# Four small moves in a sparse-attention and MoE kernel: two key loads between two row moves, three attention products one group sooner

## The chip, the cores and the metric

The kernel runs on one core of one Trainium2 chip. The metric is the device time of one execution in microseconds (us). Inside the core, TensorE (PE in the profile) multiplies, VectorE (DVE), ScalarE (ACT) and GpSimd (POOL) work on tiles, and SyncE (SP) only issues transfers (DMAs). Each engine takes its instructions strictly in the order in which the program wrote them, and waits at an instruction until what it needs has arrived.

## What is computed

Sparse attention over 4 batches, 8 heads, 768 positions and 64 features per head, and then a two-layer expert on the result. Each query sees the keys less than 16 positions away, and one summary key and value for each block of 32 positions (the maximum of the keys, the mean of the values):

```python
k_sum = k.reshape(B, H, nb, block, D).max(axis=3)
v_sum = v.reshape(B, H, nb, block, D).mean(axis=3)
scores_l = where(abs(pos_q - pos_k) < 16, scale * q @ k.T, -1e9)
scores_s = scale * q @ k_sum.T + log(block)
a = softmax(concat([scores_l, scores_s]))
x = a @ concat([v, v_sum])               # then heads side by side: 3072 x 512
h = x @ w_in                             # 512 -> 2048
out = (h * sigmoid(beta * h)) @ w_out    # 2048 -> 512
```

## The kernel before

**Tiles.** The 8 heads are taken as 4 pairs. The 768 queries of a batch are 12 tiles of 64, in two halves u of 6. For one tile the scores stand with the keys on the partitions: rows 0 to 95 are the window of 96 keys, rows 96 to 119 the 24 summary keys. `scores` (L323) fills a half for both heads of a pair in one of the three double PSUM banks `big`, ACT takes the exponential of it into a tile `e` (`weigh`, L332), and DVE multiplies `e` by the band mask (`mask_e`, L337). `av_mm` (L406) then multiplies 24 small tiles of a half: the slice of `e` is the loaded weight, and the values with a column of ones stream through; in the text a pair's two halves are AV(pair, 0) and AV(pair, 1). `norm` (L432) on DVE divides by the sum (a reciprocal and a product) and writes `xn`, and `x_dma` (L465) is a transposing DMA on ACT's queue from `xn` into `xT`, where the expert's first product reads it.

**Values.** A window of an even query tile lies at other rows than that of an odd one, so the values exist twice: `ve` for even tiles, and `vo`, the same rows shifted by 64. For batches 1 to 3, `v_cast` (L343, POOL) casts a pair into `ve`, and `v_odd_dma` (L354), the "row moves" of the pair, are two DMAs on SP's queue: L355 copies rows 64 to 127 of `ve` to rows 0 to 63 of `vo`, L356 copies rows 0 to 31 to rows 64 to 95. The summary values come from TensorE (`vm_all`, L384), and `spread` (L394, DVE) copies them into rows 96 to 127 of `vo` and of `ve`, two pairs at a time: spread(0) for pairs 0 and 1, spread(1) for pairs 2 and 3, each as two copies into `vo` and then two into `ve`. Row move L355 of a pair reads rows of `ve` (64 to 127) that spread overwrites (96 to 127), so the copies of spread(1) into `ve` wait until the row moves L355 of pairs 2 and 3 have landed.

**Loads.** `key_load` (L94) brings one pair's keys of a later batch (384 KB) by SP's queue into a staging tile `kst`; POOL and DVE cast it during the next stage.

**Order.** Nothing is scheduled by a tool: `run` (L551) takes a list of main steps and a list of side steps with positions, and writes a side step with position x behind main step floor(x), in rising order of x. In the stage around the change the main steps are the 24 groups of the second expert product of batch 0 (`o_atom`, L534): 6 tiles of 128 tokens, 4 groups each, 4 products of 128x512 in a group. The side steps are all of batch 1's attention: casts and row moves of the values, the eight score halves, masks, spreads, the four AV blocks (`av_at`, L680, pair 0 at 12.12 in `big[0]`, pairs 1, 2, 3 at 16.1 to 16.3 in `big[1]`, `big[2]`, `big[0]`), their x transposes, and the key loads of batch 2. The first expert product of batch 1 (`h_tile`, L516) follows on TensorE.

Of the kernel before, what the change touches and what calls it, by code (L numbers as in the profile page):

```python
# [11 lines left out]
def kernel(  # L12
# [57 lines left out]
    def pair(a, b, g):  # L70
        return a[b, 2 * g:2 * g + 2]
# [22 lines left out]
    def key_load(b, g):  # L94
        f = stage.tile([RK, 2, CK * D], f32, name="kst", tag="kst")
        stg[("k", b, g)] = f
        nc.sync.dma_start(out=f[:], in_=pair(k, b, g).rearrange("h (p c) d -> p h (c d)", c=CK))
# [186 lines left out]
    def km_pe(g, ks):  # L284
        key_max_win(g)
        key_sums(ks, g)
# [50 lines left out]
    def mask_e(b, g, u):  # L337
        e = et[(b, g, u)]
        return nc.vector.tensor_mul(out=e.rearrange("p h (m q) -> p h m q", q=QT), in0=e.rearrange("p h (m q) -> p h m q", q=QT),  # L339
                             in1=mask[:, None, u * HT:(u + 1) * HT, :].to_broadcast([P, 2, HT, QT]))  # L340
# [53 lines left out]
    def spread(gg):  # L394
        r = slice(NK, P)
        s = slice(2 * gg, 2 * gg + 2)
        for tt in (vo, ve):
            for h in range(2):
                nc.vector.tensor_copy(out=tt[r, s, h * J6:(h + 1) * J6, 0:D],
                                      in_=vm_sb[r, h, s, None, :].to_broadcast([P - NK, 2, J6, D]))  # L400
# [5 lines left out]
    def av_mm(b, g, u, t):  # L406
        tv = t[:, 0:AVW].rearrange("p (j h e) -> p j h e", j=3, h=2)
        e = et[(b, g, u)]
        for j in range(3):
            J = 3 * u + j  # L410
            for h in range(2):
                for par in range(2):
                    lo = (2 * j + par) * QT
                    nc.tensor.matmul(tv[par * QT:(par + 1) * QT, j, h], e[:, h, lo:lo + QT],  # L414
                                     (vo if par else ve)[:, g, h * J6 + J, 0:D + 1], start=True, stop=True)
# [16 lines left out]
    def norm(b, g, t, us):  # L432
        t = t[:, 0:len(us)]
        n = len(us)
        if us[0] == 0:
            xn[(b, g)] = xp.tile([P, J6, 2, D], bf16, name="xn", tag="xn")
        x = xn[(b, g)]
        tv = t[:, :, 0:AVW].rearrange("p k (a e) -> p k a e", e=D + 1)
        r = xp.tile([P, n, 6], f32, name="r", tag="r")
        nc.vector.reciprocal(out=r[:], in_=tv[:, :, :, D])  # L440
        nc.vector.tensor_mul(out=x[:, 3 * us[0]:3 * us[0] + 3 * n].rearrange("p (k j) h d -> p k (j h) d", k=n),  # L441
                             in0=tv[:, :, :, 0:D], in1=r[:, :, :, None].to_broadcast([P, n, 6, D]))
# [22 lines left out]
    def x_dma(b, g):  # L465
        nc.scalar.dma_start_transpose(out=xT[:, g, :].rearrange("p (j t) -> p j t", j=J6),
                                    in_=xn[(b, g)].rearrange("p j h d -> p (j h d)"))
# [83 lines left out]
    def run(main, sides):  # L551
        sides = sorted(sides, key=lambda x: x[0])
        for i, f in enumerate(main):
            f()
            while sides and sides[0][0] < i + 1:
                sides.pop(0)[1]()
        for _, f in sides:
            f()
# [84 lines left out]
    s = []  # L643
    wo = []

    def scale4(p, eng=None):
        for n in range(4 * p, 4 * p + 4):
            scale_w_out(n, eng)
# [26 lines left out]
    s = [(6, lambda: scale4(1)), (12, lambda: scale4(2)), (.5, clear_kw), (14, lambda: km_pe(0, nc.gpsimd))]  # L675
# [4 lines left out]
    def av_at(b, s, pos, bufs):  # L680
        for g in range(G):
            def av(g=g):
                for u in range(2):
                    av_mm(b, g, u, big[bufs[g]][:, u])
                norm(b, g, big[bufs[g]], [0, 1])
                if g == 0 and b > 1:
                    for u in range(2):
                        last_mask[b] = mask_e(b, G - 1, u)
            s.append((pos[g], av))

    def x_pe2(b, g, t):
        t = t.bitcast(bf16)[:, 0, 0:S]
        x = xn[(b, g)]
        for j in range(J6):
# [3 lines left out]
    s = [(.05, exp_table), (.15, lambda: scale4(3)), (.2, lambda: km_pe(1, nc.gpsimd)),  # L698
         (.3, lambda: km_pe(2, nc.gpsimd)), (3.52, lambda: km_pe(3, nc.gpsimd))]
# [10 lines left out]
    s.append((9.06, lambda: vm_all(one[1], [dve_cp] * 4)))  # L710
    s.append((9.1, lambda: spread(0)))
    s.append((9.11, lambda: spread(1)))
    av_at(1, s, [12.12, 16.1, 16.2, 16.3], [0, 1, 2, 0])
    for g in range(G):
        s.append(((12.2, 16.35, 16.4, 16.5)[g], lambda g=g: x_dma(1, g)))
    for g in range(G):
        s.append(((3.56, 3.561, 3.562, 3.563)[g], lambda g=g: key_load(2, g)))
    run(main, s)


# [3 lines left out]
    for b in range(1, B):  # L724
        n = b + 1
        s = []
# [22 lines left out]
        s = [((x[0] - 16) * 1.2, x[1]) for x in late]  # L749
# [53 lines left out]
```

## Time and profile before

| | us |
|---|---|
| median of 3 runs | 214.59 |
| fastest and slowest of them | 213.94 and 214.81 |
| the profiled execution, its whole time | 214.21 |
| its span, first to last instruction | 212.5 |
| TensorE busy in the span | 205.4 |
| VectorE, ScalarE, GpSimd busy | 110.0, 106.8, 53.8 |

Positions in the trace are us from the start of the span. A row of the timeline gives start, length, engine, line and operation of neighbouring instructions taken together, and in brackets how long the engine was idle before them and what ended that. For a DMA the row's length is the time that the issuing engine spent on it; how long after the start of the issue the data had arrived is told apart from it, as "to landing".

### The profile page before, as it was taken

What the parts mean: (1) busy time and instruction counts of PE and PEld (TensorE: products, weight loads), DVE (VectorE), ACT (ScalarE), POOL (GpSimd) and SP (SyncE); (2) the same over time, 40 slices, a digit from 0 to 9 for tenths busy, and PEclk for the clock granted to TensorE, in tenths of its full rate; (3) what the DMA queues carried; (4) which work ended last, traced back from release to release, by engine and by line L of the source; (5) the groups of instructions that cost most, each with busy time, mean ns of one, the idle gap of its engine ahead of it and who ended that gap; (6) DMA issues with size and microseconds to landing.
All of it is one profiled execution on the core that took longest, in us unless ns stands there. A gap on an engine that the chain in (4) does not pass through costs nothing.

```text
span 212.5 us, 5283 instructions
## 1 busy us (share of the span) xinstructions
PE 205.4 (97%) x2231; PEld 120.6 (57%) x2231; DVE 110.0 (52%) x251; ACT 106.8 (50%) x142; POOL 53.8 (25%) x85
## 2 busy tenths in 40 slices
PE   7997999999999999999999999999999999999993
PEld 7776766665455455665555456654554556654452
DVE  5669675398758623942798217635887100002121
ACT  2478586686756027669541066676450076640000
POOL 7949970003411203543103013343000000000000
PEclk9999999999999999999999999999999999999999
DMA  6999999999969989999579999999445400001212
GB/s 125 188 220 176 173 201 206 207 207 170 204 195 238 258 204 220 207 208 161 134 215 258 224 206 233 158 219 179 137 123 121 142 0 0 0 3 49 99 52 96
DMA packets 74534, 34.08 MB, mean 160 GB/s; under 512 B 61440, under 2 KB 70032, under 8 KB 74512
## 3 DMA queue, kind: packets, MB, share of 16 engines
q1 hardware_dynamic: 57440, 24.05, 51.8%
q0 software_dynamic: 7440, 7.34, 21.6%
q10 hardware_dynamic: 9632, 2.37, 7.5%
q8 instruction: 17, 0.28, 0.6%
q14 instruction: 5, 0.04, 0.1%
HBM read 27.37 MB, written 6.29 MB: 158 GB/s over the span
## 4 chain that ended last, share of the span: by engine, by line
PE 89%; DVE 3%; DMA 3%; POOL 2%; issue 1%; POOLq 0%; DVEq 0%
PE one L526 39%; PE big L509 29%; PE big L495 5%; PE one L501 3%; DMA qrow<-in_q_dram 3%; PE big L414 2%; PE big L328 2%; PE big L501 2%; PE big L276 1%; DVE qn L247 1%; PE one L388 1%; POOL krow L87 1%; PE big L315 0%; PE big L260 0%; DVE ve L344 0%
## 5 line engine op out<-in xcount | busy, mean ns | idle before, releaser
L526 PE MATMUL one<-w_out_sb,h_sb 128*128 128x512 bf16 (+1 forms) x400 | 85.8, 371 | 0.0
L521 ACT ACTIVATE h_sb<-big,beta_sb 128x768 bf16<-128x768 f32 x48 | 42.6, 900 | 47.5 <-PE big L509 47.5
L509 PE MATMUL big<-xT,w_in_sb 128*128 128x384 bf16 x384 | 63.1, 326 | 0.0
L526 PEld LDWEIGHTS <-h_sb 128*128 128x128 bf16 x400 | 38.1, 98 | 41.3 <-issue 0.2
L509 PEld LDWEIGHTS <-w_in_sb 128*128 128x128 bf16 x384 | 37.6, 98 | 25.3 <-issue 0.2
L247 DVE COPY o_sb<-one 128x512 f32<-128x512 f32 x19 | 13.1, 690 | 45.2 <-PE one L526 45.0
L335 ACT ACTIVATE e<-big,bias 128x768 bf16<-128x768 f32 x32 | 26.5, 897 | 16.1 <-PE big L328 13.5
L339 DVE TENSOR_TENSOR e<-e,mask 128x768 bf16<-128x768 bf16 x27 | 15.4, 594 | 14.8 <-ACT e L335 14.6
L247 DVE COPY kw<-kT 128x960 bf16<-128x960 bf16 (+1 forms) x16 | 10.2, 683 | 14.2 <-DMA kT<-kn 14.2
L344 POOL CAST ve<-vst 128x832 bf16<-128x832 f32 x15 | 13.6, 905 | 13.7 <-DMA vst<-in_v_dram 10.4
L475 POOL CAST qn<-qst 128x768 bf16<-128x768 f32 x8 | 6.6, 826 | 29.4 <-DMA qst<-in_q_dram 27.7
L241 POOL COPY kw<-km 128x288 bf16<-128x288 bf16 x12 | 7.1, 603 | 26.9 <-DVE km L233 26.9
L441 DVE TENSOR_TENSOR xn<-big,r 128x768 bf16<-128x768 f32 (+1 forms) x13 | 12.0, 927 | 0.4
L495 PE MATMUL big<-xT,w_in_sb 128*128 128x384 bf16 x64 | 11.5, 326 | 0.0
L233 DVE TENSOR_REDUCE km<-kw 128x24 bf16<-128x768 bf16 x12 | 11.3, 947 | 0.3
L641 ACT ACTIVATE h_sb<-big,beta_sb 128x384 bf16<-128x384 f32 x16 | 8.1, 579 | 2.7 <-PE big L495 2.7
L483 POOL CAST kn<-kst 96x1024 bf16<-96x1024 f32 x4 | 4.1, 1037 | 21.1 <-DVE e L339 19.1
L501 PEld LDWEIGHTS <-w_in_sb 128*128 128x128 bf16 x64 | 6.2, 98 | 4.1
L543 PE MATMUL one<-blank 128*128 128x128 bf16 (+1 forms) x98 | 7.0, 235 | 1.3 <-DVE blank L125 1.3
L501 PE MATMUL one<-xT,w_in_sb 128*128 128x384 bf16 x44 | 8.1, 326 | 0.0
L495 PEld LDWEIGHTS <-w_in_sb 128*128 128x128 bf16 x64 | 5.9, 98 | 3.6
L247 DVE COPY kw<-big 128x960 bf16<-128x960 bf16 (+1 forms) x8 | 5.3, 733 | 4.7 <-PE big L276 4.7
(126 smaller groups left out, 186.9 us busy)
## 6 DMA issues: line engine op xcount, KB each, us to landing
out_dram<-o_sb SPq DMA_DIRECT2D x23, 256.0 KB, 2.5
vst<-in_v_dram SPq DMA_DIRECT2D x13, 336.0 KB, 4.6
kst<-in_k_dram SPq DMA_DIRECT2D x8, 384.0 KB, 5.7
qst<-in_q_dram SPq DMA_DIRECT2D x8, 384.0 KB, 4.1
w_in_sb<-in_moe_w_in_dram POOLq DMA_DIRECT2D x4, 512.0 KB, 7.2
w_out_sb<-in_moe_w_out_dram POOLq DMA_DIRECT2D x4, 512.0 KB, 14.3
vo<-ve SPq DMA_DIRECT2D x12, 107.2 KB, 2.4
vst<-in_v_dram SPq DMA_DIRECT2D x3, 416.0 KB, 6.9
```

What stands on the lines that cost most here:

```text
L233: nc.vector.tensor_reduce(out=km[g][:, NK:NK + nb].rearrange("p (m n) -> p m n", n=2), in_=kw[g][:, :, W:W + QT].rearrange("p m (n f) -> p ...
L247: nc.vector.tensor_copy(out=o, in_=i)
L335: return nc.scalar.activation(out=e[:], in_=s[:, :, 0:HS], func=ACTF.Exp, bias=bias[:, 0:1], scale=scale)
L339: return nc.vector.tensor_mul(out=e.rearrange("p h (m q) -> p h m q", q=QT), in0=e.rearrange("p h (m q) -> p h m q", q=QT), in1=mask[:, No ...
L344: eng.tensor_copy(out=ve[:, g, lo:hi, 0:D], in_=vst[g][:, lo:hi])
L441: nc.vector.tensor_mul(out=x[:, 3 * us[0]:3 * us[0] + 3 * n].rearrange("p (k j) h d -> p k (j h) d", k=n), in0=tv[:, :, :, 0:D], in1=r[:, ...
L495: nc.tensor.matmul(t[:, 0:HS], w_in_sb[:, ki, i * P:(i + 1) * P], xT[:, ki, 0:HS], start=(ki == 0), stop=(ki == k1 - 1))
L501: nc.tensor.matmul(t[:, 0:HS], w_in_sb[:, ki, i * P:(i + 1) * P], xT[:, ki, lo:lo + HS], start=(ki == 0), stop=(ki == k1 - 1))
L509: nc.tensor.matmul(t[:, kk, 0:HS], w_in_sb[:, ki, i * P:(i + 1) * P], xT[:, ki, kk * HS:(kk + 1) * HS], start=(ki == 0), stop=(ki == k1 - 1))
L521: nc.scalar.activation(out=h_sb[:, i, :].rearrange("p (k m) -> p k m", k=2), in_=t[:, :, 0:HS], func=ACTF.Silu, scale=beta_sb[:, i:i + 1])
L526: nc.tensor.matmul(t[:, 0:hi - lo], h_sb[:, n, ms * P:(ms + 1) * P], w_out_sb[:, n, lo:hi], start=(n == 0), stop=(n == k2 - 1))
L641: nc.scalar.activation(out=h_sb[:, i, 0:HS], in_=t[:, i % 2, 0:HS], func=ACTF.Silu, scale=beta_sb[:, i:i + 1])
```

## The change

Two edits of positions in the list of side steps of batch 0's second expert product:

```diff
-    av_at(1, s, [12.12, 16.1, 16.2, 16.3], [0, 1, 2, 0])
+    av_at(1, s, [12.12, 15.1, 15.2, 15.3], [0, 1, 2, 0])
     for g in range(G):
-        s.append(((12.2, 16.35, 16.4, 16.5)[g], lambda g=g: x_dma(1, g)))
+        s.append(((12.2, 15.35, 15.4, 15.5)[g], lambda g=g: x_dma(1, g)))
     for g in range(G):
-        s.append(((3.56, 3.561, 3.562, 3.563)[g], lambda g=g: key_load(2, g)))
+        s.append(((3.46, 3.47, 3.562, 3.563)[g], lambda g=g: key_load(2, g)))
```

The row moves of batch 1 stand at 2.885, 2.895, 3.45 and 3.55. So on SP's queue the key loads of batch 2's pairs 0 and 1 now stand ahead of the two row moves of pair 3, and those of pairs 2 and 3 behind them as before. On TensorE the 72 products of the AV blocks of pairs 1 to 3 stand ahead of the four products of group 16 instead of behind them. The order of instructions on VectorE, ScalarE and GpSimd is the same in both kernels: the norms and the x transposes keep their places among their neighbours there.

## The prediction

> **What bounds the kernel now.** I read the page first, then the chain of work that ended last between 63 and 80 us (the stage of the change), then the busy time by stretches from there to the last products. Columns of the chain are start, length, what.
>
> ```profile
> PE 205.4 (97%) x2231; PEld 120.6 (57%) x2231; DVE 110.0 (52%) x251; ACT 106.8 (50%) x142; POOL 53.8 (25%) x85
> ```
>
> ```profile
> 63.91 0.50 PE big L414 x24
> 64.41 3.56 PE one L526 x16
> 67.97 1.26 PE big L414 x72
> 69.23 6.15 PE one L526 x28
> 75.38 3.90 PE big L509 x24
> 79.28 0.01 issue
> ```
>
> ```profile
> 167.00:209.00 42.00, 42.00 (x243) 23.50 (x240) 4.58 (x7) 14.23 (x16) 0.00 (x0) 1.00 0.11 41
> sum 145.20, PE 145.18 PEld 79.77 DVE 65.52 ACT 65.38 POOL 23.20; mean PE 16.13 PEld 8.86 DVE 7.28 ACT 7.26 POOL 2.58
> ```
>
> TensorE is the bound, and not by an average: from 63.80 to 209.00 us it is busy 145.18 of 145.20 us, at a granted clock of 1.00 (third column from the right). The chain through the stage is TensorE alone: AV of pair 0, 16 products, AV of pairs 1 to 3 (72 small products, 1.26 us), 28 products, then the next stage's first products without a gap. Two things follow. A transfer or an engine that comes sooner can save at most 145.20 - 145.18 = 0.02 us here, since nothing waits that could stop waiting. And whatever makes TensorE wait in this stage moves the end by its full length, since there is no idle time behind it that could take it up.
>
> So the question is only whether the new order makes TensorE wait. AV needs masked `e` tiles, hence DVE. Here is DVE's timeline of the stage, and SP's:
>
> ```profile
> 60.87 1.22 DVE L247 CAST vm_sb<-one 32x128 bf16<-32x128 f32 x4 [2.89 <-ACT e L335]
> 62.12 0.63 DVE L399 COPY vo<-vm_sb 32x768 bf16<-32x768 bf16 x2
> 62.67 0.62 DVE L399 COPY ve<-vm_sb 32x768 bf16<-32x768 bf16 x2
> 63.22 0.62 DVE L399 COPY vo<-vm_sb 32x768 bf16<-32x768 bf16 x2
> 63.76 0.62 DVE L399 COPY ve<-vm_sb 32x768 bf16<-32x768 bf16 x2
> 64.42 1.50 DVE L339 TENSOR_TENSOR e<-e,mask 128x768 bf16<-128x768 bf16 x3
> 65.94 0.23 DVE L440 RECIPROCAL r<-big 128x12 f32<-128x12 f32 x1
> 66.21 0.96 DVE L441 TENSOR_TENSOR xn<-big,r 128x768 bf16<-128x768 f32 x1
> 67.08 1.02 DVE L339 TENSOR_TENSOR e<-e,mask 128x768 bf16<-128x768 bf16 x2
> 68.54 0.23 DVE L440 RECIPROCAL r<-big 128x12 f32<-128x12 f32 x1 [0.43 <-PE big L414]
> ```
>
> ```profile
> 57.02 1.22 SPq L532 DMA_DIRECT2D out_dram<-o_sb  x1
> 58.41 0.48 SPq L355 DMA_DIRECT2D vo<-ve  x1
> 58.94 0.59 SPq L356 DMA_DIRECT2D vo<-ve  x1
> 59.70 0.47 SPq L355 DMA_DIRECT2D vo<-ve  x1
> 60.22 0.60 SPq L356 DMA_DIRECT2D vo<-ve  x1
> 60.86 2.06 SPq L97 DMA_DIRECT2D kst<-in_k_dram  x4
> 63.03 0.86 SPq L532 DMA_DIRECT2D out_dram<-o_sb  x2
> ```
>
> DVE works without a pause from 60.87 to 68.10: spread(0) (62.12, 62.67), spread(1) (63.22, 63.76), three masks (pair 1's second half, both of pair 2), the norm of pair 0, the two masks of pair 3, the last ending at 67.08 + 1.02 = 68.10. Only then does it wait for TensorE (0.43 us). DVE is 52% busy over the span, but here it is nearly as late as TensorE, and that share doesn't show it.
>
> **Part 1: AV one group sooner, alone.** No instruction is added; 72 products change places with 4. A product of the group takes 3.56 / 16 = 0.2225 us, so after pair 0's AV (ends 64.41) come 12 products, 2.67 us, and AV of pair 1 starts at 67.08 instead of 67.97. One pair takes 1.26 / 3 = 0.42, a half 0.21: AV(1,0) 67.08, AV(2,0) 67.50, AV(3,0) 67.92, AV(3,1) 68.13, end 68.34. The masks that they need end by DVE's row at about 64.98 (pair 1), 65.46 and 65.92 (pair 2), 67.64 and 68.10 (pair 3); `big[0]` is free for pair 3 when the norm of pair 0 ends, 66.21 + 0.96 = 67.17. Everything is in time, the last mask by 0.03 us. With some 0.05 us from DVE's end to TensorE's start (an estimate, of the size of the gaps in DVE's own rows) that costs 0.02 us; I bound it by 0 and 0.15. The gain is nothing: the x transposes go out sooner, but they are waited for by nobody:
>
> ```profile
> L466 ACTq DMA_TRANSPOSE xT<-xn x12: 1227/1272/2087, 67.2 to 162.8; - x12
> DMA to landing us min/median/max: 2.7/3.9/8.4
> ```
>
> ```profile
> 69.80 3.99 ACTq L466 DMA_TRANSPOSE xT<-xn x3
> ```
>
> The last of the three is issued until 73.79, and the products of the next stage at 75.38 wait 0.01 us. The other thing that this edit does is to spend the slack that DVE had: 0.89 us less between a mask and its reader.
>
> **Part 2: two key loads ahead of pair 3's row moves.** SP's issue time is the same in sum: two loads (2.06 / 4 = 0.52 us each) go before two row moves (0.47 and 0.60). The stores and the loads of pairs 2 and 3 behind them are issued when they were. The loads themselves gain nothing: batch 2's keys are cast only after the last mask of this stage. What moves is the arrival of the row moves, and DVE waits for the first of them: the copies of spread(1) into `ve` (63.76) overwrite rows 96 to 127, which L355 of pair 3 still reads. When did it arrive before, and the loads behind it? Each fence is one transfer, the row and its time to landing:
>
> ```profile
> L355 SPq DMA_DIRECT2D vo<-ve x1: 470/470/470, 59.7 to 59.7; - x1
> DMA to landing us min/median/max: 2.1/2.1/2.1
> ```
>
> ```profile
> L97 SPq DMA_DIRECT2D kst<-in_k_dram x1: 587/587/587, 60.9 to 60.9; - x1
> DMA to landing us min/median/max: 4.2/4.2/4.2
> ```
>
> ```profile
> L97 SPq DMA_DIRECT2D kst<-in_k_dram x1: 448/448/448, 61.5 to 61.5; - x1
> DMA to landing us min/median/max: 5.2/5.2/5.2
> ```
>
> Before, the row move landed at 59.70 + 2.1 = 61.8, 1.96 us ahead of its reader at 63.76, with nothing in front of it in the queue. The first load landed at 60.86 + 4.2 = 65.1, the second at 61.5 + 5.2 = 66.7: 5.84 us after the issue of the first. Now the first load is issued where the row move was, at about 59.6 (58.94 + 0.59 and a gap), so the second lands at 59.6 + 5.84 = 65.45, and the row move is behind both. Does a small transfer land behind a large one that was issued ahead of it by the same queue? The same queue shows it some us earlier, the last value load and pair 0's row move:
>
> ```profile
> L104 SPq DMA_DIRECT2D vst<-in_v_dram x1: 733/733/733, 53.6 to 53.6; - x1
> DMA to landing us min/median/max: 4.4/4.4/4.4
> ```
>
> ```profile
> L355 SPq DMA_DIRECT2D vo<-ve x1: 542/542/542, 54.5 to 54.5; - x1
> DMA to landing us min/median/max: 4.5/4.5/4.5
> ```
>
> The load landed at 53.61 + 4.4 = 58.0, the row move at 54.45 + 4.5 = 58.95, in order and 0.95 us apart, though alone it would have needed 2.1. So pair 3's row move lands 0.2 to 0.95 us after 65.45; the low end is two row moves of nearly one size following each other (59.70 + 2.1 = 61.8 and 60.22 + 2.0, some 0.4, and less where both had stood ready). I take 0.6: 66.05, and DVE goes on at 66.1 instead of 63.76. **The shift d is 2.3 us**; by the ends, 65.45 + 0.2 and 65.45 + 0.95, it is 1.9 to 2.7, and if the first two loads alone run a fifth faster than with two more and a store close behind them (5.84 becomes 4.7), 0.8 to 1.6.
>
> **Where d goes.** Behind the waiting copy on DVE stand spread's second copy, the five masks, the norm of pair 0: all of DVE's chain moves by d. Pair 1's second mask would end at 64.98 + 2.3 = 67.28, its reader AV(1,1) stands at 67.29: 0 to 0.1 us. Pair 2's masks end at 67.76 and 68.22, readers at 67.50 and 67.71: TensorE waits some 0.5 us in all. Pair 3's masks end at 69.94 and 70.40 (the norm of pair 0 lies between), so AV(3,1) starts at about 70.45 and ends at 70.66 instead of 68.34. TensorE waits 2.3 us in sum, in pieces of at most 1.5. In general the stall is d + 0.02 us. Without the AV edit the readers would stand 0.89 later and the stall would be about 1.4: the two edits meet in the same wait. AV of pair 0 (63.91) is not touched, since its masks, spread(0) and row moves are ahead of the wait.
>
> Is anything else late behind it? The norms of pairs 1 to 3 follow at 1.13 us each, so the last `xn` is ready at about 73.8 and its transpose issued until 75.1; landing takes 3.9 in the median from its start. The next stage's products begin at 75.38 + 2.3 = 77.7 and need the last pair's `xT` 16 of them later (16 x 0.1625 = 2.6), at 80.3. In time by 2.6 us for a median landing. No other stall, and nothing that makes the 2.3 us good, by the 145.18 of 145.20.
>
> Sum: 214.21 (the profiled execution) + 0.02 + 2.3 = 216.5. The median of the three runs shown is 0.38 above that execution, so the same sum on the median is 216.9. I say 216.7, between the two.
>
> **Rivals.**
> - *The row moves are not held up* (the transfers share the engines instead of queueing). Then the row move lands at 60.7 + 2.1 = 62.8, ahead of 63.76, d is 0, only the 0.02 to 0.15 us of part 1 are left: 214.2 to 214.7, not slower. The point from which it decides is a landing at 63.7. For it: the moves are small beside a key load, and no row shows a key load followed by a row move. Against it: the two rows above, a value load followed by one. The Trainium skill ("DMA: Bandwidth & Descriptors", "Queues, rings and completion order") says that completion is not in order for one issuing engine, and by that rule the small move could pass; it also says that each DMA engine takes its descriptors in ring order and that the closing count lands behind all earlier writes of that engine, by which it couldn't. The rows agree with the second half. Chance 0.09.
> - *A gain*: AV sooner shortens the way to the next stage. It would have to be in idle time of TensorE, and of that there is 0.02 us; on the median's own scatter (213.94 to 214.81) a time below 213.5 would need something outside this stage. 213.2. Chance 0.03.
> - *More than the queue*: the loads land later than they did, because pair 3's moves and two more loads press behind them, or an x transpose needs its 8.4 us maximum: 75.1 - 1.3 + 8.4 = 82.2 against 80.3, a second stall of 1.9 us. 214.6 + 2.3 + 1.0 to 1.9, 217.9 to 218.8. Chance 0.07.
>
> **How the numbers follow.** The queue delay has a chance of 0.81: with d from 0.8 to 2.7 on 214.21 to 214.59 it gives 215.0 to 217.3, most of it above 215.7. The range is 215.2 to 217.7, which leaves out the first two rivals, most of the third and the lowest corner of the first case. 0.5% is 1.07 us, about what a measurement of this kernel can tell from no change. Slower by more than that: nearly all of the 0.81 and the 0.07, less 0.04 for a d under 1.07, 0.84. Within it: 0.09 + 0.04 = 0.13. Faster: 0.03.
>
> **What would show it.** In the changed kernel's trace: the L355 move of pair 3 issued near 60.7 and landing after the second key load, near 66; DVE idle some 2.3 us before a copy into `ve`, ended by a DMA; TensorE idle in front of AV of pairs 2 and 3, put down to DVE's masks, in sum about d; all later rows moved by that much and no new idle time. If that DVE wait is absent and the time is up all the same, my mechanism is wrong; if the wait is there and TensorE doesn't stall, the slack was mis-sized.

## The result, and the profile after

| | before | changed |
|---|---|---|
| median of 6 runs, us | 214.70 | 216.42 |
| fastest and slowest | 213.94 and 215.07 | 216.06 and 217.54 |
| profiled execution, its time and span | 214.21, 212.5 | 216.38, 214.6 |

The changed kernel takes 1.0086 times as long, with a 95% interval of 1.0057 to 1.0115: 1.85 us more (1.2 to 2.5). The sum of the prediction was 2.3 more, the time given 216.7.

The profile shows first whether TensorE now waits. The stretch of the stage in both kernels, before and then after; the first pair of numbers is the length and TensorE's busy time:

```profile
63.80:72.00 8.20, 8.20 (x134) 4.47 (x127) 7.57 (x17) 3.74 (x5) 2.02 (x2) 1.00 1.09 222
```

```profile
63.80:72.00 8.20, 6.45 (x137) 3.91 (x130) 6.29 (x14) 3.76 (x5) 1.78 (x2) 1.00 0.79 211
```

By this row it is idle 1.75 us where it was idle 0.00, at an unchanged clock of 1.00. (Of the 1.75, two pauses of 0.16 us put down to "issue" stand next to rows of 11 and 31 products where e1_av_only's chain below has 12 and 32; they may well be missing records rather than pauses.) Who it waits for is in the waits of the changed kernel between 56 and 82 us (engine, line, whom, us in all, times, longest):

```profile
PEld L414 <- DVE e L339: 1.7, 2, 1.5
PE big L414 <- DVE e L339: 1.3, 1, 1.3
```

The weight loads and products of AV (L414) wait for masked tiles, as forecast. SP's and DVE's timelines of the changed kernel show why the masks are late:

```profile
58.92 0.48 SPq L355 DMA_DIRECT2D vo<-ve  x1
59.45 0.60 SPq L356 DMA_DIRECT2D vo<-ve  x1
60.09 1.07 SPq L97 DMA_DIRECT2D kst<-in_k_dram  x2
61.34 0.47 SPq L355 DMA_DIRECT2D vo<-ve  x1
61.85 0.59 SPq L356 DMA_DIRECT2D vo<-ve  x1
```

```profile
63.44 0.62 DVE L399 COPY vo<-vm_sb 32x768 bf16<-32x768 bf16 x2
65.81 0.63 DVE L399 COPY ve<-vm_sb 32x768 bf16<-32x768 bf16 x2 [1.75 <-DMA vo<-ve]
66.47 1.50 DVE L339 TENSOR_TENSOR e<-e,mask 128x768 bf16<-128x768 bf16 x3
67.99 0.23 DVE L440 RECIPROCAL r<-big 128x12 f32<-128x12 f32 x1
68.26 0.96 DVE L441 TENSOR_TENSOR xn<-big,r 128x768 bf16<-128x768 f32 x1
69.14 1.01 DVE L339 TENSOR_TENSOR e<-e,mask 128x768 bf16<-128x768 bf16 x2
```

Read the bracket of the second row: DVE, which had no pause here before, stands 1.75 us in front of spread(1)'s copies into `ve`, and a DMA from `ve` into `vo` ends it. The whole chain behind it (masks, norm, masks) moves with it. The times to landing, first of the two key loads (the first has the least, the second the most), then of pair 3's first row move:

```profile
L97 SPq DMA_DIRECT2D kst<-in_k_dram x2: 448/516/583, 60.1 to 60.7; - x2
DMA to landing us min/median/max: 3.7/4.2/4.7
```

```profile
L355 SPq DMA_DIRECT2D vo<-ve x1: 475/475/475, 61.3 to 61.3; - x1
DMA to landing us min/median/max: 4.3/4.3/4.3
```

The second load landed at 60.72 + 4.7 = 65.4, the row move at 61.34 + 4.3 = 65.6; alone it needed 2.1. The chain that ended last then shows the way into TensorE:

```profile
61.34 4.35 DMA vo<-ve
...
69.22 0.94 DVE e L339 x2
70.16 0.04 issue
70.21 0.38 PE big L414 x12
70.59 0.16 issue
70.75 6.85 PE one L526 x31
77.60 3.90 PE big L509 x24
```

Last mask 70.16, AV(3,1) 70.21, then the remaining products and the next stage without another wait for an engine. Only the last halves are late: measured from start to start of its products in TensorE's timeline, AV(2,1) comes 0.2 us, AV(3,0) 1.5 us and AV(3,1) 0.3 us later than it would behind its neighbour, 2.0 us in all. That is more than the idle time of the stretch because the rows of these products are 0.2 us long though the products start 0.03 us apart in twos, and the last row in front of a wait counts as busy to its end. So that the start of a run, which shifts everything by some tenths of a us from one execution to the next, doesn't blur the comparison, I measure each kernel's stage inside its own trace: from the first AV product of pair 0 to the first product of the next stage. Before, 63.84 to 75.22, 11.38 us; changed, 64.05 to 77.44, 13.39 us. The difference of 2.01 us is nearly all of the 2.1 us of span.

### The profile page after: what moved, and what is told of

Same layout as the page of the kernel before. It is cut to its first block, busy times and chain, and to the rows that moved or that the text cites. A ratio compares the mean times of both kernels' runs of the same rounds, so it can differ in the third digit from the quotient of the medians.

```text
span 214.6 us, 5266 instructions
## 1 busy us (share of the span) xinstructions
PE 204.5 (95%) x2214; PEld 120.9 (56%) x2231; DVE 110.3 (51%) x251; ACT 107.0 (50%) x142; POOL 53.7 (25%) x85
## 4 chain that ended last, share of the span: by engine, by line
PE 77%; DVE 9%; DMA 6%; POOL 3%; issue 2%; SPq 1%; POOLq 0%; DVEq 0%
PE one L526 32%; PE big L509 29%; PE big L495 5%; DMA qrow<-in_q_dram 3%; DVE kw L247 2%; DMA vo<-ve 2%; DMA vst<-in_v_dram 2%; PE big L414 2%; PE big L328 2%; DVE w_out_sb L216 2%; DVE e L339 1%; PE one L501 1%; POOL ve L344 1%; DVE km L233 1%; DVE xn L441 1%
## 5 line engine op out<-in xcount | busy, mean ns | idle before, releaser
L526 PE MATMUL one<-w_out_sb,h_sb 128*128 128x512 bf16 (+1 forms) x383 | 83.4, 370 | 1.9 <-issue 1.4
L509 PEld LDWEIGHTS <-w_in_sb 128*128 128x128 bf16 x384 | 37.6, 98 | 25.3 <-issue 0.2
L247 DVE COPY o_sb<-one 128x512 f32<-128x512 f32 x19 | 13.1, 690 | 45.8 <-PE one L526 45.7
L247 DVE COPY kw<-kT 128x960 bf16<-128x960 bf16 (+1 forms) x16 | 10.2, 682 | 14.2 <-DMA kT<-kn 14.2
L501 PEld LDWEIGHTS <-w_in_sb 128*128 128x128 bf16 x64 | 6.2, 98 | 4.1
L414 PEld LDWEIGHTS <-e 128*64 128x64 bf16 x336 | 6.3, 111 | 3.7 <-DVE e L339 2.0
L247 DVE COPY kw<-big 128x960 bf16<-128x960 bf16 (+1 forms) x8 | 5.3, 732 | 5.1 <-PE big L276 5.1
```

The source lines that it names most:

```text
L247: nc.vector.tensor_copy(out=o, in_=i)
L501: nc.tensor.matmul(t[:, 0:HS], w_in_sb[:, ki, i * P:(i + 1) * P], xT[:, ki, lo:lo + HS], start=(ki == 0), stop=(ki == k1 - 1))
L509: nc.tensor.matmul(t[:, kk, 0:HS], w_in_sb[:, ki, i * P:(i + 1) * P], xT[:, ki, kk * HS:(kk + 1) * HS], start=(ki == 0), stop=(ki == k1 - 1))
L526: nc.tensor.matmul(t[:, 0:hi - lo], h_sb[:, n, ms * P:(ms + 1) * P], w_out_sb[:, n, lo:hi], start=(n == 0), stop=(n == k2 - 1))
```

## The experiments

Theory A is the one of the prediction: two key loads in the queue ahead of pair 3's row moves, DVE stopped by the first of these, masks late for AV, and the AV edit taking away the slack that would have covered half of it. Rival B gives each edit a price of its own that adds up; rival C puts the loss down to the loads' traffic, whatever DVE waits for. All times are against the kernel before on the same chip; "stage" is the stretch defined above, less 11.38, from one profile. The last two kernels ran once each, next to a single run of the kernel before, so that they have no interval, and their times (214.34 and 218.98 us, before 217.19) are not compared.

| kernel | ratio (95% interval) | us more | stage, us more | DVE's wait at spread(1), us |
|---|---|---|---|---|
| changed | 1.0086 (1.0057 to 1.0115) | 1.85 | 2.01 | 1.75 |
| e1_av_only | 1.0014 (0.9998 to 1.0029) | 0.3 | 0.17 | 0 |
| e2_keys_only | 1.0051 (1.0029 to 1.0073) | 1.1 | 0.91 | 1.52 |
| e3_one_key | 1.0016 (0.9997 to 1.0035) | 0.3 | 0.16 | 0 |
| e4_spread_late | 1.0021 (1.0000 to 1.0042) | 0.45 | 0.40 | 0 |
| e5_four_keys | 1.0338 (1.0309 to 1.0366) | 7.3 | 7.24 | 5.22 |
| e6_act_queue | 1.0006 (0.9992 to 1.0021) | 0.1 | 0.16 | 0 |
| e7_spread_mid | 1.0045 (1.0022 to 1.0069) | 1.0 | 0.55 | 0.20 |
| e8_av_later | 1.0051 (1.0028 to 1.0074) | 1.1 | 0.00 | 1.03 |
| e9_act_behind | 1.0015 (0.9976 to 1.0055) | 0.3 | 0.17 | 0 |
| e10_three_keys | 1.0267 (1.0208 to 1.0327) | 5.7 | 5.56 | 4.15 |
| e11_act_later | one run | | 0.17 | 0 |
| e12_act_last | one run | | 4.38 | 2.59 |

### Each edit alone

**e1_av_only**: the changed kernel with the key loads where they were.

```diff
-        s.append(((3.46, 3.47, 3.562, 3.563)[g], lambda g=g: key_load(2, g)))
+        s.append(((3.56, 3.561, 3.562, 3.563)[g], lambda g=g: key_load(2, g)))
```

> Theory A (one wait: pair 3's row move lands behind two key loads, VectorE stops at the copy into ve, its masks come late for AV of pairs 2 and 3): the AV blocks one group sooner alone only spend slack; the last mask is 0.02 us short, so 0.0 to +0.15 us against before. Rival B (each edit has a price of its own and the two add up to the 1.7 to 1.9 us measured): about +0.9 us. Rival C (the key loads' traffic, sooner in the stage, slows the stage whatever VectorE waits for): 0.0.

Measured +0.3 us (-0.04 to +0.6), 0.17 in the stage: rival B's 0.9 is out. The chain that ended last has it in one row, AV of pairs 1 to 3, which was 1.26:

```profile
65.28 2.70 PE one L526 x12
67.98 1.43 PE big L414 x72
69.41 7.01 PE one L526 x32
```

Where the 0.17 us arise shows in TensorE's timeline, at the last product of AV(3,0) and the first of AV(3,1). The last mask ended at 67.96 + 1.02 = 68.98:

```profile
68.85 0.20 PE L414 MATMUL big<-vo,e 128*64 128x65 bf16 x1
69.03 0.22 PE L414 MATMUL big<-ve,e 128*64 128x65 bf16 x1
```

The products before them start in twos, 0.03 us apart; this step takes 0.18.

**e2_keys_only**: the kernel before with the key loads of the change.

```diff
-        s.append(((3.56, 3.561, 3.562, 3.563)[g], lambda g=g: key_load(2, g)))
+        s.append(((3.46, 3.47, 3.562, 3.563)[g], lambda g=g: key_load(2, g)))
```

> Theory A: VectorE is shifted by 1.8 us as in the changed kernel, of which 0.87 us is slack when AV stands where it stood: +0.95 us against before (0.6 to 1.3), the wait of VectorE for the row move unchanged at about 1.75 us in the profile. Rival B: the rest to 1.85 after the first experiment, about +0.9 us, the same here. Rival C: all of it, +1.7 to +1.9 us.

Measured +1.1 us (0.6 to 1.6), 0.91 in the stage. DVE's wait is nearly the changed kernel's, and TensorE's is a third of it (one row of each engine's timeline):

```profile
65.74 0.63 DVE L399 COPY ve<-vm_sb 32x768 bf16<-32x768 bf16 x2 [1.52 <-DMA vo<-ve]
```

```profile
69.67 0.22 PE L414 MATMUL big<-ve,e 128*64 128x65 bf16 x1 [0.45 <-DVE e L339]
```

The stages don't add up as rival B wants (0.17 + 0.91 = 1.08, not 2.01): the same late masks cost more when their reader comes 0.89 us sooner. This rests on the stages of single profiles: the times alone (0.3 and 1.1 alone, 1.85, between 1.2 and 2.5, together) don't tell a sum from more than a sum. Rival C's 1.7 to 1.9 lies outside the interval.

### The queue, dose by dose

**e3_one_key** and **e5_four_keys**: the changed kernel with one and with four key loads ahead of pair 3's row moves; **e10_three_keys** with three.

```diff
-        s.append(((3.46, 3.47, 3.562, 3.563)[g], lambda g=g: key_load(2, g)))
+        s.append(((3.46, 3.561, 3.562, 3.563)[g], lambda g=g: key_load(2, g)))   # e3
+        s.append(((3.46, 3.47, 3.48, 3.49)[g], lambda g=g: key_load(2, g)))      # e5
+        s.append(((3.46, 3.47, 3.48, 3.563)[g], lambda g=g: key_load(2, g)))     # e10
```

> Only pair 0's key load ahead of pair 3's row moves, AV sooner. Theory A: in the changed kernel the first load landed 1.6 us before the second, at 63.8; the row move lands 0.25 us behind it, near 64.0 to 64.3, against a reader that is ready at 64.0: VectorE waits 0 to 0.4 us, +0.0 to +0.4 us against before. Rivals B and C (a price for each load): about half of what the loads cost, with AV sooner +0.9 to +1.4 us.

With one load ahead the row move still landed later than alone (60.26 + 3.8 = 64.1), but ahead of its reader:

```profile
L355 SPq DMA_DIRECT2D vo<-ve x1: 470/470/470, 60.3 to 60.3; - x1
DMA to landing us min/median/max: 3.8/3.8/3.8
```

```profile
64.30 0.62 DVE L399 COPY ve<-vm_sb 32x768 bf16<-32x768 bf16 x2
```

No bracket, no wait, and 0.16 us in the stage, what the AV edit costs alone. It is not a price for each load: the first is free, the second costs nearly all.

> All four key loads of batch 2 ahead of pair 3's row moves, AV sooner. Theory A: two more loads are ahead in the queue, which in the kernel before landed 2.8 us after the second one; the row move lands at about 68.4 and VectorE waits 4.4 to 4.9 us: +4.2 to +5.0 us against before. Rival C (traffic moved ahead, the same in sum): about as the changed kernel, +1.7 to +2.2 us.

Measured +7.3 us, well above the 4.2 to 5.0 of theory A, though the direction was right and DVE's wait nearly so:

```profile
L355 SPq DMA_DIRECT2D vo<-ve x1: 475/475/475, 61.8 to 61.8; - x1
DMA to landing us min/median/max: 7.8/7.8/7.8
```

```profile
69.70 0.63 DVE L399 COPY ve<-vm_sb 32x768 bf16<-32x768 bf16 x2 [5.22 <-issue]
```

The row move landed at 61.79 + 7.8 = 69.6 and DVE went on at 69.70 (the bracket names "issue" here; the landing is what fits). DVE's 5.22 us are 0.3 above the upper end. The other 2 us are in the stretches of TensorE (length, busy; the clock is the third column from the right):

```profile
66.00:68.00 2.00, 2.00 (x21) 0.86 (x18) 0.00 (x0) 1.59 (x3) 0.00 (x0) 1.00 1.07 269
68.00:71.00 3.00, 0.07 (x6) 0.03 (x2) 1.27 (x4) 0.00 (x0) 0.00 (x0) 1.00 0.40 143
71.10:77.80 6.70, 5.52 (x68) 3.07 (x67) 6.18 (x12) 0.58 (x1) 2.02 (x2) 0.50 0.43 98
77.90:80.00 2.10, 2.10 (x11) 0.98 (x10) 0.15 (x1) 0.00 (x0) 0.00 (x0) 1.00 0.87 169
```

After a stretch of 3.00 us with 0.07 us of work the granted clock stood at 0.50 for all of the next 6.7 us. The products of the stage show it, 32 in 8.62 us in this kernel's chain, where before 28 took 6.15 (0.27 us each against 0.22):

```profile
74.64 8.62 PE one L526 x32
```

> Three of the four key loads ahead of pair 3's row moves, AV sooner. With two ahead the row move landed near 65.7, with four near 69.6. Theory A: with three it lands between, near 67 to 68, VectorE waits 2.9 to 4.0 us and the time is +2.9 to +4.2 us if TensorE keeps its full clock, as with two loads, where its longest pause was 1.3 us; +4.5 to +6 us if the clock falls as with four loads, where the longest pause was 2.9 us and the clock then stood at half for 6.8 us. The first is the likelier, since the longest pause would be about 2 us. Rival C: +1.7 to +2.2 us.

Measured +5.7 us (4.5 to 7.0): between two loads and four, as theory A has it. The row move landed at 61.92 + 6.5 = 68.4 and DVE waited 4.15 us, both above what was expected (67 to 68, and 2.9 to 4.0). And the likelier branch of the expectation was wrong, for the clock fell here too:

```profile
68.00:72.00 4.00, 1.14 (x36) 0.80 (x36) 3.37 (x8) 0.00 (x0) 0.00 (x0) 1.00 0.51 158
72.10:75.40 3.30, 2.93 (x29) 1.54 (x30) 3.20 (x8) 0.58 (x1) 2.02 (x2) 0.50 0.48 115
75.50:77.50 2.00, 2.00 (x11) 0.94 (x10) 0.78 (x1) 0.00 (x0) 0.00 (x0) 1.00 1.01 197
```

Its longest pause is 1.9 us; but over 4.00 us TensorE worked 1.14. In the changed kernel the same stretch, 68 to 72, has 2.40 us of work and the clock stays at 1.00:

```profile
68.00:72.00 4.00, 2.40 (x44) 1.51 (x44) 3.90 (x8) 0.58 (x1) 1.78 (x2) 1.00 0.54 155
```

### DVE's order instead of the queue's

**e4_spread_late** and **e7_spread_mid**: both edits kept, no transfer touched, spread(1) later among DVE's instructions.

```diff
-    s.append((9.11, lambda: spread(1)))
+    s.append((12.125, lambda: spread(1)))    # e4: behind three masks and the norm of pair 0
+    s.append((9.23, lambda: spread(1)))      # e7: behind the three masks
```

> Both edits kept; on VectorE the second spread (pairs 2 and 3) stands behind the three masks and the norm of pair 0, ahead of the two masks of pair 3. Theory A: its copies into ve come at about 67, after the landing at 65.7, so nothing waits: 0.0 to +0.3 us against before, the cost of the change gone without touching a transfer. Rivals B and C: the transfers and AV are where the changed kernel has them, so +1.7 to +1.9 us.

Measured +0.45 us (0.0 to 0.9), 0.40 in the stage. DVE's timeline has no wait left at the copies:

```profile
67.23 0.62 DVE L399 COPY ve<-vm_sb 32x768 bf16<-32x768 bf16 x2
67.88 1.03 DVE L339 TENSOR_TENSOR e<-e,mask 128x768 bf16<-128x768 bf16 x2
```

Most of the loss is gone with AV and every transfer where the change has them, so rivals B and C fall: what costs is DVE's standing at that copy. The rest, a little above the expected 0.3, is the AV edit's 0.17 and some 0.24 us by which DVE's chain from its first cast (L247) to the end of its last mask is longer in this order (7.47 against 7.23).

> As the changed kernel, with the second spread behind the three masks but ahead of the norm of pair 0. Theory A: its copies into ve are ready at 64.0 + 1.5 = 65.5, the row move lands at 65.7, so the wait shrinks from 1.75 to about 0.3 us: +0.2 to +0.5 us against before. Rivals B and C: +1.7 to +1.9 us.

```profile
66.37 0.63 DVE L399 COPY ve<-vm_sb 32x768 bf16<-32x768 bf16 x2 [0.20 <-DMA vo<-ve]
```

The wait is 0.20 us, the stage 0.55 longer, the time +1.0 us (0.5 to 1.5): the wait as expected, the time at or above the upper end of the expected 0.2 to 0.5. Of the 0.55, the wait is 0.20 and the AV edit 0.17; DVE's chain from its first cast to its last mask is longer by the remaining 0.18 without the wait (7.61 with it, against 7.23). The rest of the time's 1.0 I can't place.

### AV later, and a miss

**e8_av_later**: the key loads of the change, AV of pairs 1 to 3 and their x transposes at 17.1 to 17.5.

```diff
-    av_at(1, s, [12.12, 15.1, 15.2, 15.3], [0, 1, 2, 0])
+    av_at(1, s, [12.12, 17.1, 17.2, 17.3], [0, 1, 2, 0])
-        s.append(((12.2, 15.35, 15.4, 15.5)[g], lambda g=g: x_dma(1, g)))
+        s.append(((12.2, 17.35, 17.4, 17.5)[g], lambda g=g: x_dma(1, g)))
```

> Key loads as in the changed kernel, AV of pairs 1 to 3 and their x transposes one group later than before (two later than in the change). Theory A: VectorE still waits 1.75 us, but AV's readers have 0.89 us more slack than before: shift 1.83 less 1.76 leaves 0.0 to +0.2 us against before, if the x transposes are still in time (their margin was 1.9 us). Rival B (the price of the loads stays, that of AV turns round): +0.0 to +0.9. Rival C: +1.7 to +1.9 us.

Theory A holds inside the stage: DVE waits 1.03 us and the stage is 0.00 us longer, the wait fully covered by later readers. In this profile the wait was shorter than the 1.75 expected (SP issued the loads 0.6 us sooner than in the changed kernel's profile, 59.52 for 60.09, and DVE was ready 0.2 us later), so that the full 1.8 us of slack was not put to the test. But the time is up by 1.1 us (0.6 to 1.6), outside the expected 0.2. The next stage's first products pay a part of it, 0.63 us, in the chain and in TensorE's timeline; the rest is not placed:

```profile
73.82 5.20 DMA xT<-xn
```

```profile
79.06 1.14 PE L509 MATMUL big<-xT,w_in_sb 128*128 128x384 bf16 x6 [0.63 <-DMA xT<-xn]
```

The last x transpose was issued at 73.82 and landed 5.2 us later, where I had counted with the 3.6 us of the kernel before. That was the miss: in the changed kernel the last transpose took 5.4 us too, and between 4.0 and 5.7 in e1 to e4, e6, e7 and e9. Here it was issued 1.85 us ahead of the next stage's first product, before 2.7, which left too little margin for that.

### Another queue for the row moves

**e6_act_queue**, **e9_act_behind**, **e11_act_later**, **e12_act_last**: pair 3's row moves on ScalarE's queue, at four places in its order.

```diff
-    def v_odd_dma(g):
-        nc.sync.dma_start(...)
+    def v_odd_dma(g, q=nc.sync):
+        q.dma_start(...)
...
-        s.append(((2.885, 2.895, 3.45, 3.55)[g], lambda g=g: v_odd_dma(g)))
+        s.append(((2.885, 2.895, 3.45, 7.9)[g], lambda g=g: v_odd_dma(g, nc.scalar if g == 3 else nc.sync)))
+        # e9: 9.035   e11: 9.045   e12: 9.055
```

> As the changed kernel, but pair 3's two row moves are issued by ScalarE's queue behind its second output copy; SP issues the four key loads in a row. Theory A with the delay due to the order within one queue: the row moves overlap with the loads and land 2 to 3.5 us after their issue, by 62.7, before their reader: 0.0 to +0.3 us against before. Theory A with the delay due to shared transfer engines: they land near 64.5 to 65.7 in spite of the other queue: +0.6 to +1.8 us. Rival C: +1.7 to +1.9 us.

Measured +0.1 us (-0.2 to +0.5). But the moves were issued at 58.03 and 58.61, 1.5 us ahead of the first load, so this run says only that ahead of the loads they cost nothing, not what the queue does.

> Pair 3's row moves on ScalarE's queue again, but between its exponentials, so that they are issued near 60.7, after the key loads have begun on SP's queue (four of them, issued 59.6 to 61.6). If the delay in the changed kernel comes from the order within one queue, they land about 2 to 2.7 us after their issue, near 63 to 63.5, VectorE waits 0 us and the time is 0.0 to +0.5 us against before (ScalarE loses 1.1 us in the stage). If it comes from the shared transfer engines, they land 4 us or more after their issue, at 64.8 or later, VectorE waits 0.5 us or more, and the time is +0.5 to +3 us.

Again the first move went out at 60.94, 0.2 us ahead of the first load (61.12), and landed in 2.5 us; the second, 0.4 us behind the first load's issue, took 3.7 instead of 2.0. The time is +0.3 us (-0.5 to +1.2). A hint at sharing, no verdict.

> As the run before it on ScalarE's queue, with the two row moves one exponential later, so that at least two of SP's key loads are issued ahead of them. What is read is the landing, not the time. Order within one queue: the row moves land 2 to 2.7 us after their issue, as those without anything ahead (2.0 to 2.2). Shared transfer engines: 4 us or more, as the 4.3 us of the move behind two loads on SP's queue. Between the two: part of each.

Here too the first move was issued at 59.88, ahead of the loads (60.04), with 2.3 us to landing, and the second at 60.50, behind one load, with 3.9.

> The same with the row moves behind all three exponentials, so that all four key loads are issued ahead of them on SP's queue. Order within one queue: 2 to 2.7 us to landing. Shared transfer engines: behind four loads on SP's queue a row move took 7.8 us, issued 0.6 us after the last load; so 5 us or more.

In this run two of SP's four loads went out ahead of the first row move (59.87 and 60.49) and two behind it, fewer ahead than I had meant. SP's and ACT's timeline rows, the landing of the first row move, and DVE's row:

```profile
59.87 2.14 SPq L97 DMA_DIRECT2D kst<-in_k_dram  x4
```

```profile
60.68 0.56 ACTq L355 DMA_DIRECT2D vo<-ve  x1
```

```profile
L355 ACTq DMA_DIRECT2D vo<-ve x1: 562/562/562, 60.7 to 60.7; - x1
DMA to landing us min/median/max: 6.0/6.0/6.0
```

```profile
66.77 0.63 DVE L399 COPY ve<-vm_sb 32x768 bf16<-32x768 bf16 x2 [2.59 <-issue]
```

From another queue, with two loads issued ahead of it elsewhere, the move took 6.0 us, where from the same queue ahead of the loads it had taken 2.3 (e6 and e11) and 2.5 (e9). Behind two loads on SP's queue it took 4.3; a part of the difference is that here it was issued 0.81 us after the first load, there 1.25. DVE then waits 2.59 us, longer than in the changed kernel. So the key loads hold the move up in either queue, and the order within SP's queue alone can't be the reason; that the queues share the transfer engines fits, but what exactly is shared isn't shown. It is one profile; e9 and e11 agree in their second moves.

The stage of this run is 4.38 us longer, more than its wait explains: TensorE's longest pause was 1.34 us, as in the changed kernel, yet the granted clock stood at 0.50 from 71.0 to 74.4, and the 32 products behind AV took 8.38 us in the chain instead of 7.01 (e1).

## Why the prediction was right, and where its sizes were off

- **The bound.** TensorE had no pause to give back, and every wait moved the end: 2.01 us in the stage, 2.1 in the span. Right.
- **AV sooner, alone**: 0.02 us forecast with bounds 0 to 0.15; the stage took 0.17, just above, and the same 0.16 to 0.17 in e3, e6, e9 and e11. The 0.05 us from DVE's end to TensorE's start were right (68.98 to 69.03 in e1). What was mis-sized is when TensorE gets to the last half. (A half of a pair is 12 products; 24, as said of `av_mm` above, are a pair.) The prediction gave a half 0.21 us, a sixth of 1.26. By the starts of its products it takes 0.19, and the rest of the 1.26 is the change to the next products. So in e1 TensorE could have begun AV(3,1) at about 68.88, some 0.1 us ahead of the mask, where the prediction had it 0.03 behind the mask.
- **The second key load's landing**: 65.45 forecast, 65.4 measured, though the first was issued 0.5 us later than assumed (60.09 for 59.6) and they landed faster: the second 5.3 us after the first one's issue, not 5.84.
- **The row move behind it**: 0.6 us taken, 0.2 measured, the low end of the bounds. This is the main term that was too large. The shift d was 65.81 less the 63.98 at which the copies were ready, 1.83 for 2.3, and the stall 2.01 for 2.32: a d that was 0.5 too large and an AV term that was 0.15 too small partly made each other good. (1.83 + 0.17 = 2.00, so the form of the sum was right.) Some 0.25 of the 0.5 is that the load landed 1.4 us after DVE's copies were ready instead of 1.7; that its position came out at 65.4 as forecast is luck, a later issue against a faster landing.
- **d goes fully into TensorE**: shown by e4 and e7 (the same transfers, DVE not stopped there, most of the time back) and by e2 (without the AV edit the slack of 0.89 us is left and covers about that much; 1.4 forecast, 0.91 in the stage, with d smaller than forecast).
- **Nothing else late**: right for the change, but closer than forecast. The prediction had the last x transpose in time by 2.6 us at a median landing of 3.9; in the changed kernel it was issued at 74.0 and landed 5.4 us later, at 79.4, some 0.6 us ahead of the product that needs it (77.44 + 2.6 = 80.0). With AV two groups later, in e8, it came too late. (The 0.01 us that the prediction calls a wait of the products at 75.38 stands at 79.28 in its own row; nothing hangs on it.)
- **The rivals.** A gain: out, 1.85 us more. More than the queue: no second stall came, TensorE was busy 8.00 of 8.00 us from 72 to 80. Row moves that aren't held up: out, 4.3 us against 2.1. The Trainium skill's rule by which a later small transfer may pass ("DMA: Bandwidth & Descriptors", "Queues, rings and completion order") did not come true on SP's queue in any run here: with one to four loads ahead, pair 3's row moves landed after all loads that were issued ahead of them. (In e12, from the other queue, the second row move, issued at 61.28, landed at 67.9, some 0.2 us before the third load, issued 0.3 us ahead of it.) The reason that the prediction gave, order within one queue, is too narrow by e12. The same page's section "Issuing engines are not separate DMA queues" says that all transfers run on the same 16 engines and interleave whoever issues them; e12's 6.0 us agree. What stays open is how much of the delay either adds.

## What to carry to other kernels

Before a transfer is moved ahead of a small one in time, find the first instruction that waits for the small one, also a write that must not overwrite what it still reads: here a copy on an engine at 52% stood still for 1.75 us, and the bound engine with it. An engine's share of busy time says nothing of its slack at one place; the gap between a result and its reader does, and two edits that use up the same gap can cost more together (2.01 us in the stage) than one by one (0.17 and 0.91). Such a wait may be moved in the waiting engine's own order, without touching the transfer: here that left 0.40 of the 2.01 us (e4).

## What the runs showed of the hardware

TensorE's granted clock fell to 0.50 not only after a pause of 2.9 us (e5, for 6.8 us) but also after two pauses of 1.9 and 1.3 us with little work between (e10, 1.14 us of work in 4.00), and not with 2.40 us of work in 4.00 (the changed kernel). Nor does the longest pause decide alone: it was 1.34 us in the changed kernel, where the clock stayed at 1.00, and 1.34 in e12, where it fell to 0.50 for 3.4 us; there TensorE worked 1.56 us between 67.70 and 71.10, ahead of the fall, against 1.80 in the changed kernel between 68.00 and 71.40. Where the limit lies, these runs don't show. The Trainium skill ("TensorE: Matmul & The Clock Gate", "Part 1: The HAM clock gate") has the clock halve after an idle window of about 3.4 us; the half agrees, but pauses shorter than that were enough here. A transfer of 64 rows took 2.1 us to land with no load ahead, 3.8 behind one key load of 384 KB on its queue, 4.3 behind two, 6.5 behind three, 7.8 behind four, and 6.0 from another engine's queue with two of four loads issued ahead of it.
